# Blocks 1 to 3 of a convolution and feed-forward kernel: turning tiles by transposing transfers instead of on TensorE

## The chip, the cores and the metric

The kernel runs on one core of a Trainium2 chip. The metric is the device time of one execution in microseconds, lower is better; the tables of the profile give times from the start of the span of one profiled execution.

## The reference

One sequence of S = 2048 rows with D = 640 channels (F = 1728 in the feed-forward part). All tensors are bfloat16.

```python
x = A_q
# A: layernorm, short causal filter on k, long causal convolution, gate
q = layernorm(x)
k_shift = sum over t < 4 of k shifted by t rows * shift_k[:, t]
kv = k_shift * A_v
y = causal_convolution(kv, A_ssm_k)          # written with FFTs of length 2*S
y = y + kv * A_ssm_D                         # the skip term
h = x + q * y
# B: layernorm and a gated feed-forward
g = silu(layernorm(h) @ w_gate)
u = layernorm(h) @ w_up
out = h + (g * u) @ w_down
```

## The kernel before, in words

The sequence is cut into four blocks of 512 rows (`j` = 0 to 3); a partition holds four neighbouring rows, so a tile has 128 partitions times four rows (`b`). The channels are cut into two halves of 320 (`c`). For each block and half `conv_c` does the long convolution of the block as a product of spectra:

- `kv_block` (DVE, `tt`, L463): the four-tap filter on k and the product with v, eight products and sums of 128x1280. The rows of k come with three halo rows ahead of them: block 0 loads all channels at once (`load_kv_all`), later blocks by `load_kv`.
- `load_kraw` and `k_natural`: the long filter of the block lies in DRAM with channels as rows. It is loaded so, turned by 12 TensorE transposes of 128x128 (L557), and copied from PSUM to `kt` by ACT (L438) or DVE (L439). For block 0 POOL then adds the skip coefficients to the filter's first row (`dadd`, L564): tap zero of the convolution carries the skip term.
- `fwd`: stage one of the transform on TensorE (L454) and a copy out of PSUM for each `b`, then four shuffles within SBUF (`sh...`, L446, on SP) that bring groups of partitions together. `spec`: stage two. `swapped`: two transfers that exchange the halves of a spectrum. `prods`: products and sums of spectra of this and earlier blocks on DVE. `inv2`, four transfers `rs...`, and `conv_bp` for the way back; `conv_bp` also multiplies by the normed row and adds it to x, and takes the statistics of the second layernorm.
- `ln_bp`: the normed rows `hn` (ACT at L686 or DVE), two row blocks at a time, are turned by 10 TensorE transposes (L848) and copied into `HNT`, which holds channels as partitions.
- `ffn_pair` (seven for a block, L454 with 512 columns): two gate and two up groups of five matmuls into the PSUM tiles `g` and `u`, Silu on ACT (L892), and the product with `u` straight out of PSUM on DVE (`gm`, L463, 128x1024). `ffn_b`: the matmuls of the down projection, the sum with h, and the store.

Every operation goes through `P.op`, which records what it reads and writes. The order on each engine is not found at run time: a packed table `_ORDER` holds, for each operation, its engine and its place, and `replay` and `emit` turn that into five programs, one for each engine, with waits on semaphores. Work of one block's feed-forward and of the next blocks' convolution is interleaved in that order. An engine works strictly in its order: a wait at the head holds everything behind it. That holds for the queues as well: nearly all transfers are issued by SP (L446), a few by POOL and ACT. Buffers come from named pools (`P.pool`), and an operation that reuses a buffer waits for the readers of the earlier tile. The PSUM banks are in two pools of two tiles, `pF` (feed-forward, and part of block 0) and `pC`. Small operations of the layernorm, a power on POOL (L676) among them, stand between the statistics and `hn`.

Of the kernel before, what the change touches and what calls it, by code (L numbers as in the profile page):

```python
# [309 lines left out]
def bass_sequential_preLN__ssm_conv_h3__swiglu_ffn__prompt_kernel(  # L310
# [13 lines left out]
    RESPE = [False, False, False, False]  # L324
    FM = 1664
# [9 lines left out]
    with ExitStack() as es:  # L335
# [14 lines left out]
        def slots(n, size):  # L350
            return [alloc(size) for _ in range(n)]
# [42 lines left out]
        KR01 = P.tile("kraw01", None, WD.base)  # L394
# [7 lines left out]
        P.pool("KRAW", slots(1, 3 * B), True)  # L402
# [9 lines left out]
        P.pool("E", slots(6, HW), True)  # L412
        P.pool("PP", slots(3, HW), True)
        P.pool("EP", slots(3, 2 * CW), True)
# [30 lines left out]
        def dma(subs, kb, reads, writes, prio, eng="sp", after=(), name="", desc=1280, kids=True):  # L445
            fns = [(lambda g, d=d, s=s: g.dma_start(d(), s())) for d, s in subs]  # L446
            engs = {e: {"pool": 0.8, "act": 0.56, "sp": 0.56}[e] * len(subs) for e in ((eng,) if isinstance(eng, str) else eng)}
            return P.op(engs, fns, reads, writes, prio, after=after, dma=(kb, desc), name=name)
# [61 lines left out]
        def load_kv_all(prio):  # L510
            kt, vt = P.tile("kin0", None, GUT.base), P.tile("vin0", None, HNT.base)

            def rows(p0, p1):
                return (lambda: V(kt, 0, 7 * D, p0, p1), lambda: dram(K2, (R * p0 - 3) * D, [[R * D, p1 - p0], [1, 7 * D]]))

            P.op({"pool": 0.3}, lambda g: g.memset(V(kt, 0, 3 * D, 0, 1), 0.0), [], [(kt, "z")], prio, name="kz")
            dma([rows(16, 128), rows(1, 16), (lambda: V(kt, 3 * D, 4 * D, 0, 1), lambda: dram(K2, 0, [[R * D, 1], [1, 4 * D]]))],
                1147, [], [(kt, 0), (kt, 1)], prio, name="kin0", desc=4480)
            dma([(lambda: V(vt, 0, 4 * D), lambda: dram(V2d, 0, [[R * D, 128], [1, R * D]]))], 655, [], [(vt, 0), (vt, 1)], prio + 2, name="vin0", eng=("sp", "act", "pool"), desc=2560)
            for c in range(2):  # L520
                kins[0, c], vins[0, c] = Slab(kt, D, c * CW, c), Slab(vt, D, c * CW, c)

        def load_kv(j, c, prio):
# [3 lines left out]
                750, [], [(kt, 0)], prio, name=f"kin{j}{c}", eng=("sp", "pool"), desc=640)  # L527
            dma([(lambda: V2(vt, 0, CW, 4, CW), lambda: dram(V2d, B * j * D + c * CW, [[R * D, 128], [D, 4], [1, CW]]))],
                426, [], [(vt, 0)], prio + 1, name=f"vin{j}{c}", eng=("sp", "pool"), desc=640)

        def load_kraw(j, c, prio):
            t = kraws[j, c] = KR01 if (j, c) == (0, 1) else P.tile(f"kraw{j}{c}", "KRAW")
            base = c * CW * S + B * j
            dma([(lambda: V2(t, 0, B, 2, B), lambda: dram(A_ssm_k, base, [[S, 128], [128 * S, 2], [1, B]])),
                 (lambda: V(t, 2 * B, B), lambda: dram(A_ssm_k, base + 192 * S, [[S, 128], [1, B]]))],
                393, [], [(t, 0)], prio, name=f"kraw{j}{c}", eng=("sp", "pool") if j else ("act", "sp", "pool"), desc=1024)

        def load_x(j, prio):
            t = xts[j] = P.tile(f"x{j}", "XH")
            dma([(lambda: V(t, 0, 4 * D), lambda: dram(X2, B * j * D, [[R * D, 128], [1, R * D]]))], 655, [],  # L540
                [(t, (b, c)) for b in range(4) for c in range(2)], prio, name=f"x{j}", eng=("sp", "pool"), desc=2560)

        kts = {}
        ktrs, dadds = {}, []

        def k_natural(j, c, prio):
            kr = kraws[j, c]
            kt = P.tile(f"kt{j}{c}", "KT")
            kts[j, c] = Slab(kt, CW, 0, 0)
            pt = P.tile("pKT", cpool(j))  # L550
# [12 lines left out]
            if j == 0:  # L563
                dadds.append(P.op({"pool": 1.0}, lambda g: g.tensor_tensor(out=V(kt, 0, CW, 0, 1), in0=V(kt, 0, CW, 0, 1),  # L564
                                                                           in1=V(DROW, c * CW, CW, 0, 1), op=ALU.add),
                                  [(DROW, 0), (kt, 0)], [(kt, 0)], prio, name="dadd"))

        def fwd(j, nm, srcs, tbpool, upool, prio):

            tbt = P.tile("TB" + nm, tbpool)  # L570
            for b in range(4):
# [6 lines left out]
                pe(fns, CW, len(fns), [(s.t, s.cell) for s, _ in srcs] + [(TAB, 0)], [(pt, 0)], prio, reserve=[(tbt, b)], name=f"s1{nm}b{b}")  # L578
# [3 lines left out]
            for G in range(R):  # L582
# [3 lines left out]
                def src(G=G):  # L586
# [3 lines left out]
                    name=f"sh{nm}G{G}")  # L590
# [9 lines left out]
        def swapped(nm, src, off, h, prio):  # L600
            t = P.tile("W" + nm, "E")
            dma([(lambda: V(t, 0, HW, 0, 64), lambda: V(src, off, HW, 64, 128)), (lambda: V(t, 0, HW, 64, 128), lambda: V(src, off, HW, 0, 64))],
                328, [(src, 2 * h), (src, 2 * h + 1)], [(t, 2 * h), (t, 2 * h + 1)], prio, name=f"sw{nm}", desc=2560)
# [63 lines left out]
        def ln_rstd(l, j, prio, two_pass, bs):  # L667
            lo, hi = bs[0], bs[-1] + 1
            va, y, nm, ng = (tmv(l, j, i)[:, lo:hi] for i in (0, 2, 3, 5))
            if two_pass:  # L670
                src, k1, rd = va, 1.0 / D, [(ST, ("ss", l, j, b)) for b in bs]
            else:
                src, k1, rd = agv(l, j)[:, lo:hi], 1.0, [(ST, ("a", j, b)) for b in bs]
            c1, c3, c4 = ([(ST, ("t", l, j, i, b)) for b in bs] for i in (0, 2, 3))
            vec(0.16, lambda v: v.tensor_scalar(out=va, in0=src, scalar1=k1, scalar2=LN_EPS, op0=ALU.mult, op1=ALU.add), rd, c1, prio, name=f"va{l}{j}")  # L675
            P.op({"pool": 0.4}, lambda g: g.tensor_tensor(out=y, in0=va, in1=stt[:, 288:288 + hi - lo], op=ALU.pow), c1 + [(ST, "half")], c3, prio,  # L676
# [16 lines left out]
        def ln_dve(l, j, prio, bs):  # L693
# [5 lines left out]
            ln_rstd(l, j, prio, False, bs)  # L699

        def ln_x(j, prio):
            for b in range(4):
                for c in range(2):
                    ln_stats(0, j, b, c, xts[j], prio)
            ln_dve(0, j, prio, range(4))

        def kv_block(j, c, prio):
# [12 lines left out]
            def mul(dst, jj):  # L720
                vec(dve2(HW), tt(lambda: v4(dst), lambda: kt.rows(3 - jj), lambda: tapb(jj), ALU.mult),
                    [(kt.t, kt.cell), (kt.t, "z"), (TAPS, jj)], [(dst, 0)], prio, name=f"kvm{j}{c}")
# [15 lines left out]
        def inv2(j, c, G, p1, p2, HTt, prio):  # L738
# [14 lines left out]
            dma([(dst, lambda: V(ht, 0, 2 * CW))], 164, [(ht, 0)], [(HTt, G)], prio + 1, name=f"rs{j}{c}G{G}")  # L753
# [44 lines left out]
        def conv_bp(j, c, bp, HTt, pr):  # L798
# [9 lines left out]
            for k in range(2):  # L808
# [3 lines left out]
            vec(dve1(2 * CW), tt(lambda: V2(ot, 0, CW, 2, CW), lambda: B32x2(pt, CW), lambda: V2(qt, 0, CW, 2, CW), ALU.mult),  # L812
                [(pt, 0), (qt, 0), (qt, 1)], [(ot, 0)], pr, name=f"o{j}{c}{bp}")
# [6 lines left out]
        def conv_c(j, c):  # L820
# [4 lines left out]
            uk = fwd(j, f"K{j}{c}", srcs, "TBK", "UK", pb + 104)  # L825
# [10 lines left out]
        def ln_bp(j, bp, pr):  # L836
            xt = xts[j]
            pt = P.tile("p5", "pC")
            hn = []
            for k in range(2):  # L840
# [3 lines left out]
                norm(lambda t=t: V(t, 0, D), lambda b=b: V(xt, b * D, D), D, 1, j, b, [(xt, (b, 0)), (xt, (b, 1))], [(t, 0)], pr, f"hn{j}{b}")  # L844
            fns = []
# [3 lines left out]
            cells = [(HNT, (d, bp)) for d in range(5)]  # L849
# [5 lines left out]
        def load_weights():  # L855
# [3 lines left out]
            early = [ktrs[0, 1], dadds[1]] + tapms  # L859
# [12 lines left out]
            for w, (wd, o_) in enumerate(((B_w_up, 0), (B_w_gate, 64))):  # L872
                piece([(lambda o_=o_: V2(GUL, o_, 128, 5, 64), lambda wd=wd: dram(wd, FM, [[F, 128], [128 * F, 5], [1, 64]]))], 150,
# [5 lines left out]
        def ffn_pair(j, i, pf):  # L879
# [3 lines left out]
            hr = [(HNT, (d, bp)) for d in range(5) for bp in range(2)]  # L883

            def group(t, bank, w, st, col, cell, prio, reserve):
                fns = [mm(lambda: B32(t, bank, 512), lambda d=d: V(w, d * st + col, 128), lambda d=d: V(HNT, d * 512, 512), d == 0, d == 4)
                       for d in range(5)]
                wr = [(GUL, 0), (GUL, 1)] if w is GUL else [(w, col // 128)]
                pe(fns, 512, 5, hr + wr, [(t, cell)], prio, reserve=reserve, name=f"gu{j}{i}{bank}")
# [9 lines left out]
            if not last:  # L899
# [4 lines left out]
                mul(lambda: V2(GUT, f0 * 512, 512, 2, 512), lambda: B32x2(u, 512), lambda: V2(GUT, f0 * 512, 512, 2, 512), 1024,  # L904
                    [(u, 0), (u, 1), (GUT, f0), (GUT, f1)], [(GUT, f0), (GUT, f1)])
# [31 lines left out]
        def block_j(j):  # L937
# [12 lines left out]
            ln_x(j, pb + (300 if j else 95))  # L950
# [25 lines left out]
    "c-pN~2~?9;7A6bX_k<*5-#0=?LdXVL2q6hcAYn;>up}TNvZ-K4YaONT9a{yg7I(_At+iTgacSM!V%=!bx||lR(rVpxtk$Zis1xjJXL>wSd+$5<-T(dfegFHu"  # L976
    "cYiPd1O&zaq8^PP5O~A@05BN%gn@p|Vt}B>)lnZQ{h#>=Ao%h4!vY|>J!(Hszd{0@1rqQRBp~Luv;Ok%Qx=5*fk%i%*^Lm4iCXjoPm2HmaAX34{}6t*Kh+2D"
    "R4(9ODxV<q#Oi;udMY;XuVX*f3GiF?%nE@<#<M5{{yk~%<LmzY);}%y3%dR7UwlH%Xs7=TYJ&cbe*3eo_+wuH|8MP{iVu9O*Uu9DUMb+Of9go~j7o)K`eH&c"
    "b+pd`Zvd_XP6FgWJzyrF5ilQI71J2g9<vV61fYT<@G-zp%o%_Y@Eo`w8bo=JrBE=qJ$5m~0(*p-hMI#4VNRo=7&n#y8V%YGl7m-*Z-TR8x5W~G?*c=hFTvc{"
    "RB%~r6SyN54EBM)i={*IApqD$hyywuatPvrEP~)62xuGh0Mr1Jz}ujoK-WVXVS8Y=U^ie&_y;gC;zI-rxd(|uZ9)Q29#jT=EqpPYgNPuGBF-QP$Xdh-<SQsW"  # L980
    "dL{Z(%sey#Q-B%3euuq)b>fcU8u5n-6ha&BM_dcRMii2Ih#-g;vJ*mt&Vt^CdSI`^>SLjhPKX3v55Ea7MMx2^A;R#p@G}S+awcj!Di_s)>Ok&5y@q%RxdV}d"
    "grY6zN$8g`^(YNmiyA`7F_$ovm<^b2bT0NGwjQ?wXTW#i?%*cimtut2Tj)%T2Aht12OEnUhZW+l;j;-HgfoQMgrfu&v7dMeFD5M^N#mBq^~Tkaj*-46`QskO"
    "O(MTVz8rTaZZ&xvc`^A*@*}c?(n*m}50MASCW@9)LRmoRqp+!4sHyRTWFTo6(@yH39c52|&4+Zcn>qXFm!*8pPVxojZpb`ZU%Zh~LEl1$GM6)l7-rTx>`s=P"
    "lfx0PQQSq`LmUzh%h&RngoDCX{#?-|ey@Npeo<r-t`QH5XGs=GQ)FN%H{qrXDeX_Vm#{*5T3VJ^ASWim6lqGAcD+KAgi*FC&#OLCYLj;*Z`R<nPSqExR&{G~"
    "TuL6W1HKj*LcWcc;rt*jb|P{k<{a`8dKmW=YCTRtIgjrnEWvN1PNA=+QyG_G$?$pbLHKwC5Q#=X(1Va+s1LgWyAxA^-HEpowiB?#5V4)uM|_h!4gW6wI4&7)"
    "!#CmmxE9<HUP-7S7)et|fH-g53vohXAX?i-+#9DQpCe~dzM(9kOrY+iisN63KN`O%elY$E+S_q6$T;d4Y8k16)JEP-evitHpA~;ReiiKkO+}wW2Qvy77Ur9b"
# [46 lines left out]
```

## Time and profile before

| | |
|---|---|
| median of 13 runs | 325.06 us (323.07 to 328.06) |
| the profiled execution's own time | 323.07 us |
| its span | 321.3 us |
| mean granted TensorE clock | 0.967 |
| HBM read, written | 20.63 MB, 2.62 MB |
| moved by all queues | 49.78 MB |
| transfers issued by SP, POOL, ACT | 217, 13, 4 |
| L557 transposes of the filter | 96, in 8 batches of 12 |
| L848 transposes of the normed rows | 80, in 8 batches of 10 |
| copies of 128x1280 out of PSUM | 10 on ACT (1232 ns), 6 on DVE (820 ns) |

The busy time of an engine is a union of overlapping instructions. For TensorE a busy stretch need not be one at full pace: matmuls are pipelined, and their modelled ends include the way through the array. The number of matmuls in a stretch times their pace in a stretch where nothing holds them says more. A wait is put down to the last of its releasers.

### The profile page before, as it was taken

The numbers are of one execution on the slowest core, as the hardware profiler recorded it, in microseconds if no ns is written. First come the engines' busy times: TensorE is split into PE (matmuls) and PEld (weight loads), VectorE is DVE, ScalarE is ACT, GpSimd is POOL, SyncE is SP. The second block draws the span as 40 slices with busy tenths as digits, with TensorE's granted clock in tenths as the row PEclk, the third lists the DMA queues.
The fourth block names the chain that finished last, engine by engine and source line by source line (L and its number), as shares of the span: only waits on it lengthen the run. The fifth ranks groups of instructions, "written<-read, shape, count | busy, mean of one in ns | idle before, by whom it ended". The sixth has DMA issues, their size and how long they took to land.

```text
span 321.3 us, 4710 instructions
## 1 busy us (share of the span) xinstructions
PE 277.2 (86%) x1650; PEld 156.7 (49%) x1668; DVE 251.2 (78%) x423; ACT 172.8 (54%) x245; POOL 28.5 (9%) x34
## 2 busy tenths in 40 slices
PE   3368487648999698999999999989999999999992
PEld 1243143324454454677555456754444576444671
DVE  1499889897985998999999989989998885123421
ACT  3168579984989475647577577672545302321100
POOL 2110010230240010020000020030001001000000
PEclk9999859976999999999999999999999999999999
DMA  7957969797979468347633601647441110000001
GB/s 204 382 189 228 303 226 286 243 303 228 286 237 289 127 213 228 108 119 241 199 131 104 196 30 71 185 136 226 121 104 42 42 43 10 33 0 0 2 20 62
DMA packets 39355, 49.78 MB, mean 155 GB/s; under 512 B 4466, under 2 KB 33347, under 8 KB 39205
## 3 DMA queue, kind: packets, MB, share of 16 engines
q1 hardware_dynamic: 37682, 45.17, 46.2%
q0 software_dynamic: 1088, 3.88, 4.0%
q10 hardware_dynamic: 562, 0.43, 0.6%
q8 instruction: 13, 0.21, 0.3%
q14 instruction: 10, 0.08, 0.1%
HBM read 20.63 MB, written 2.62 MB: 72 GB/s over the span
## 4 chain that ended last, share of the span: by engine, by line
PE 54%; DVE 15%; ACT 11%; DMA 10%; issue 5%; POOL 2%; SPq 1%; ACTq 0%; DVEq 0%
PE ps L454 52%; DVE sb L463 12%; ACT sb L438 8%; DMA sb<-sb 8%; DMA sb<-in_A_ssm_k_dram 3%; POOL stt L676 2%; DVE stt L660 2%; SPq L446 1%; PE ps L848 1%; PE ps L557 1%; ACT sb L892 1%; ACT sb L686 1%; ACT sb L441 0%; ACT L892 0%; DVE stt L664 0%
## 5 line engine op out<-in xcount | busy, mean ns | idle before, releaser
L454 PE MATMUL ps<-sb 128*128 128x512 bf16 (+2 forms) x978 | 189.7, 343 | 4.0 <-DMA sb<-in_A_shift_k_dram 2.2
L463 DVE TENSOR_TENSOR sb<-sb 128x1280 bf16<-128x1280 bf16 (+1 forms) x208 | 158.5, 793 | 9.3 <-DMA sb<-sb 4.7
L454 PEld LDWEIGHTS ps<-sb 128*128 128x128 bf16 (+1 forms) x996 | 97.0, 98 | 76.6 <-DMA sb<-in_A_shift_k_dram 2.2
L438 ACT ACTIVATE sb<-ps 128x640 bf16<-128x640 f32 (+1 forms) x140 | 97.7, 745 | 53.3 <-PE ps L454 50.1
L454 PE MATMUL ps<-sb,tab 128*128 128x320 bf16 x496 | 94.7, 325 | 24.3 <-DMA sb<-sb 8.0
L463 DVE TENSOR_TENSOR sb<-ps,sb 128x640 bf16<-128x640 f32 (+3 forms) x64 | 60.6, 950 | 37.0 <-PE ps L454 35.7
L454 PEld LDWEIGHTS ps<-sb,tab 128*128 128x128 f16 x496 | 47.2, 103 | 67.3 <-DVE sb L463 11.6
L892 ACT ACTIVATE sb<-ps 128x1024 bf16<-128x1024 f32 (+2 forms) x32 | 29.3, 917 | 41.8 <-PE ps L454 41.7
L686 ACT ACTIVATE sb<-sb,stt 128x320 bf16<-128x320 bf16 (+1 forms) x40 | 28.3, 734 | 17.1 <-DVE stt L678 15.3
L660 DVE BATCH_NORM_STATS2 stt<-sb 128x6 f32<-128x320 bf16 x64 | 29.7, 481 | 0.1
L441 ACT ACTIVATE sb<-ps 128x640 bf16<-128x640 f32 x31 | 21.2, 702 | 12.6 <-PE ps L454 12.5
L676 POOL TENSOR_TENSOR stt<-stt 128x2 f32<-128x2 f32 (+1 forms) x12 | 14.6, 1224 | 149.9 <-DVE stt L675 107.2
L557 PE MATMUL ps<-sb 128*128 128x128 bf16 x96 | 8.5, 253 | 7.3 <-issue 6.0
L439 DVE COPY sb<-ps 128x1280 bf16<-128x1280 bf16 x6 | 4.9, 820 | 10.5 <-PE ps L557 7.9
L557 PEld LDWEIGHTS ps<-sb 128*128 128x128 bf16 x96 | 7.5, 125 | 9.6 <-issue 9.1
L848 PE MATMUL ps<-sb 128*128 128x128 bf16 x80 | 6.9, 242 | 2.6 <-ACT sb L686 2.0
L848 PEld LDWEIGHTS ps<-sb 128*128 128x128 bf16 x80 | 5.5, 109 | 5.0 <-ACT sb L686 3.2
L446 POOL DMA_DIRECT2D sb<-in_A_ssm_k_dram x6 | 4.1, 680 | 41.8 <-PE ps L557 24.2
L664 DVE BATCH_NORM_AGGREGATE stt<-stt 128x2 f32<-128x12 f32 x32 | 5.5, 191 | 0.0
L678 DVE TENSOR_TENSOR stt<-stt 128x2 f32<-128x2 f32 (+1 forms) x12 | 1.8, 155 | 4.5 <-POOL stt L676 4.3
L439 DVE CAST sb<-ps 128x640 bf16<-128x640 f32 x2 | 1.6, 825 | 3.3 <-PE ps L454 3.3
L564 POOL TENSOR_TENSOR sb<-sb 1x320 bf16<-1x320 bf16 x2 | 2.0, 1014 | 17.1 <-DVE sb L439 10.5
(19 smaller groups left out, 19.0 us busy)
## 6 DMA issues: line engine op xcount, KB each, us to landing
sb<-sb SPq DMA_DIRECT2D x160, 160.0 KB, 2.6
sb<-in_A_k_dram SPq DMA_DIRECT2D x6, 560.0 KB, 5.7
sb<-in_A_q_dram SPq DMA_DIRECT2D x4, 640.0 KB, 4.7
out_dram<-sb SPq DMA_DIRECT2D x16, 160.0 KB, 1.9
sb<-in_A_v_dram SPq DMA_DIRECT2D x5, 320.0 KB, 3.7
sb<-in_B_w_gate_dram SPq DMA_DIRECT2D x3, 480.0 KB, 4.6
sb<-in_A_ssm_k_dram SPq DMA_DIRECT2D x4, 256.0 KB, 5.0
sb<-in_A_k_dram SPq DMA_DIRECT2D x1, 980.0 KB
```

The costliest lines, as they stand in the source:

```text
L438: fns = {"act": lambda a: a.activation(out=dst(), in_=src(), func=ACTF.Copy), "dve": lambda v: v.tensor_copy(out=dst(), in_=src())}
L439: "dve": lambda v: v.tensor_copy(out=dst(), in_=src())}
L441: fns = {"act": lambda a: a.activation(out=dst(), in_=src(), func=ACTF.Copy, scale=scale), "dve": lambda v: v.tensor_scalar(out=dst(), in0 ...
L446: fns = [(lambda g, d=d, s=s: g.dma_start(d(), s())) for d, s in subs]
L454: return lambda t: t.matmul(o(), l(), r(), start=st, stop=sp)
L463: return lambda v: v.tensor_tensor(out=o(), in0=a(), in1=b_(), op=op)
L557: return t.transpose(B16(pt, b // 2, (b % 2) * CW + o_, 128), src, V(IDN, 0, 128))
L660: vec(dve1(CW, False), lambda v: v.bn_stats(st6(l, j, b, c), V(xt, b * D + c * CW, CW)), [(xt, (b, c))], [(ST, ("s", j % 2, b, c))], prio, ...
L676: P.op({"pool": 0.4}, lambda g: g.tensor_tensor(out=y, in0=va, in1=stt[:, 288:288 + hi - lo], op=ALU.pow), c1 + [(ST, "half")], c3, prio, ...
L686: "act": lambda a: a.activation(out=dst(), in_=src(), func=ACTF.Identity, scale=rs(l, j, b), bias=tmv(l, j, 3)[:, b:b + 1])},
L848: fns.append(lambda t, k=k, d=d: t.transpose(B16(pt, k, d * 128, 128), V(hn[k], d * 128, 128), V(IDN, 0, 128)))
L892: P.op({"act": act_c(n)}, lambda a: a.activation(out=dst(), in_=src(), func=ACTF.Silu), rd, wr, -1000, name=f"si{j}{i}")
```

## The change

The filters of blocks 1 to 3 and the normed rows of blocks 1 to 3 are turned by `dma_start_transpose` on SP; block 0 keeps the TensorE transposes. A turned filter lands with row 128a + p in partition p, so four more transfers inside SBUF bring it to four neighbouring rows a partition. The skip term of block 0 enters stage one as a matmul with one row. Block 0's own rows of k come in one transfer and the halo rows in two others after it. In `ffn_pair` of blocks 0 to 2, the `u` tile of the first six pairs is copied to SBUF by ACT, and the product reads SBUF. The first pair of block 0 is done in halves of 256 columns, so that its first half needs only the first two row blocks. Some shuffles of block 0 may be issued by ACT, three are. Pools `E` (five buffers, six before), `PP` and `EP` are no longer handed out in strict order, `UT` is new, `KN` replaces `KRAW`. The packed order is a new one: engines and places of operations change throughout, and so do the queues of some loads (x of blocks 0 and 2 and one piece of the transform's table on POOL, most of the weights on SP, issued later).

```diff
+    HNX = [False, True, True, True]
+    SPLIT = ((0, 0),)
+    UEV = [(0, 1, 2, 3, 4, 5), (0, 1, 2, 3, 4, 5), (0, 1, 2, 3, 4, 5), ()]
+    OEV = [False] * 4
...
-        P.pool("KRAW", slots(1, 3 * B), True)
+        P.pool("KN", slots(1, HW), True)
...
-        P.pool("E", slots(6, HW), True)
-        P.pool("PP", slots(3, HW), True)
-        P.pool("EP", slots(3, 2 * CW), True)
+        P.pool("UT", slots(1, 1024))
+        P.pool("E", slots(5, HW))
+        P.pool("PP", slots(3, HW))
+        P.pool("EP", slots(3, 2 * CW))
...
@@ load_kv_all
-            dma([rows(16, 128), rows(1, 16), (lambda: V(kt, 3 * D, 4 * D, 0, 1), lambda: dram(K2, 0, [[R * D, 1], [1, 4 * D]]))],
-                1147, [], [(kt, 0), (kt, 1)], prio, name="kin0", desc=4480)
+            dma([(lambda: V(kt, 3 * D, 4 * D), lambda: dram(K2, 0, [[R * D, 128], [1, R * D]]))], 655, [], [(kt, 0), (kt, 1)], prio, name="kin0", desc=5120)
+            dma([halo(16, 128), halo(1, 16)], 491, [], [(kt, "h")], prio, name="kinh", desc=3840)
...
@@ load_kraw
+            if j:
+                t = kraws[j, c] = P.tile(f"kn{j}{c}", "KN")
+                P.op({"sp": 0.6}, [lambda g: g.dma_start_transpose(V2(t, 0, CW, 4, CW), dram(A_ssm_k, base, [[S, CW], [1, B]]))],
+                     [], [(t, 0)], prio, dma=(328, 1024), name=f"kx{j}{c}")
+                return
...
@@ k_natural
+            if j:
+                dma([(lambda a=a: V2(kt, 0, CW, 4, CW, 32 * a, 32 * a + 32), lambda a=a: V(kr, a * CW, CW)) for a in range(4)],
+                    328, [(kr, 0)], [(kt, 0)], prio, name=f"shk{j}{c}", desc=640)
+                return
...
-            if j == 0:
-                dadds.append(P.op({"pool": 1.0}, lambda g: g.tensor_tensor(out=V(kt, 0, CW, 0, 1), in0=V(kt, 0, CW, 0, 1),
-                                                                           in1=V(DROW, c * CW, CW, 0, 1), op=ALU.add),
-                                  [(DROW, 0), (kt, 0)], [(kt, 0)], prio, name="dadd"))
...
@@ fwd
+                if skip is not None and b == 0:
+                    fns = [mm(lambda T=T, pt=pt: B32(pt, T, CW), lambda T=T: tb(oS1 + T * 128, 128, 0, 1),
+                              lambda: V(DROW, skip * CW, CW, 0, 1), True, False) for T in range(2)] + [
+                           mm(lambda T=T, pt=pt: B32(pt, T, CW), lambda T=T: tb(oS1 + T * 128, 128), lambda: srcs[0][0].row(0), False, True)
+                           for T in range(2)]
...
@@ kv_block
-                    [(kt.t, kt.cell), (kt.t, "z"), (TAPS, jj)], [(dst, 0)], prio, name=f"kvm{j}{c}")
+                    [(kt.t, kt.cell)] + ([(kt.t, "h"), (kt.t, "z")] if jj else []) + [(TAPS, jj)], [(dst, 0)], prio, name=f"kvm{j}{c}")
...
@@ ln_bp
+            if HNX[j]:
+                for k in range(2):
+                    b = bp * 2 + k
+                    P.op({"sp": 0.6}, [lambda g, b=b, k=k: g.dma_start_transpose(V2(HNT, b * 128, 512, 5, 128), V(hn[k], 0, D))],
+                         [(hn[k], 0)], [(HNT, (d, b)) for d in range(5)], pr, dma=(164, 1280), name=f"hx{j}{b}")
+                return
...
@@ ffn_pair
+                cuts = ((0, 256), (256, 512)) if (j, i) in SPLIT else ((0, 512),)
...
+                if i in UEV[j]:
+                    ut = P.tile("ut", "UT")
+                    P.op({"act": act_c(1024)}, lambda a: a.activation(out=V(ut, 0, 1024), in_=B32x2(u, 512), func=ACTF.Copy),
+                         [(u, 0), (u, 1)], [(ut, 0)], -1000, name=f"ue{j}{i}")
+                    vec(dve2(1024), tt(gv, gv, lambda: V(ut, 0, 1024), ALU.mult), [(ut, 0)] + gc, gc, -1000, name=f"gm{j}{i}")
...
 _ORDER = (
-    "c-pN~2~?9;7A6bX_k<*5-#0=?LdXVL2q6hcAYn;>up}TNvZ-K4YaONT9a{yg7I(_At+iTgacSM!V%=!bx||lR(rVpxtk$Zis1xjJXL>wSd+$5<-T(dfegFHu"
+    "c-p;E2UyeB7AJe}y~rYikOcvfkU@4r0)d1iK!C^wCt3&YQH$+U>p-oF+PbxFY^{Qd1MRR+sjW|6>!_oCKC4f0TdDe@wbuIT_xio|y>sq8_uTV8-|zm<?;J1y"
...
```

## The prediction

> **What bounds the kernel now.** I read the page's busy rows first, then the table of stages, then the chain of waits, then the groups by form.
>
> ```profile
> PE 277.2 (86%) x1650; PEld 156.7 (49%) x1668; DVE 251.2 (78%) x423; ACT 172.8 (54%) x245; POOL 28.5 (9%) x34
> PEclk9999859976999999999999999999999999999999
> ```
> ```profile
> 12.00:41.00 29.00, 18.13 (x85) 8.62 (x84) 27.56 (x44) 17.92 (x27) 2.03 (x2) 0.93 0.84 261
> 41.00:73.00 32.00, 21.40 (x120) 10.49 (x119) 29.12 (x64) 28.51 (x44) 6.10 (x7) 0.82 0.87 266
> 73.00:107.00 34.00, 29.59 (x168) 16.10 (x171) 27.90 (x41) 24.76 (x35) 6.16 (x7) 0.92 0.89 257
> 107.00:144.00 37.00, 35.55 (x235) 21.91 (x239) 35.51 (x58) 22.81 (x33) 3.67 (x4) 1.00 0.51 150
> 144.00:183.00 39.00, 38.79 (x239) 22.03 (x241) 38.56 (x58) 25.73 (x33) 0.83 (x2) 1.00 0.57 178
> 183.00:216.00 33.00, 32.07 (x226) 20.94 (x226) 30.86 (x62) 23.52 (x36) 4.74 (x3) 1.00 0.36 110
> ```
> Columns of the stages: length, then PE, weight load, DVE, ACT and POOL busy, granted clock, DMA share, GB/s. From 107 us PE and DVE are both nearly full; before that DVE is, PE is not.
>
> ```profile
> 1.22 8.21 DMA sb<-in_A_ssm_k_dram
> 9.43 1.25 issue
> 10.67 1.46 PE ps L557 x12
> 12.15 0.06 DVE sb L439
> ...
> 33.72 6.10 DMA sb<-sb
> ...
> 111.43 0.67 PE ps L557 x12
> ...
> 146.50 0.56 PE ps L848 x10
> ...
> 250.76 16.80 PE ps L454 x117
> ...
> 281.97 10.74 PE ps L454 x49
> ```
> Busy PE time overlaps itself, so I take the paces of the chain instead: 49 matmuls of 512 columns in 10.74 us is 0.219 us each, 117 (nearly all of 320 columns) in 16.80 us is 0.144; with bare pitches of 0.216 and 0.136, and 0.056 for a transpose (0.56 us for 10), the matmuls counted in each stage come to 9.5 of 29 us, 14.6 of 32, 26.5 of 34, and then 202.8 of the 209 us from 107 to 316. So the kernel is a front of 107 us in which PE is starved of about 54 us, and a stretch in which PE is the limit with DVE close behind. A change gains if it takes work off PE in the stretch, or lets the front hand over earlier.
>
> ```profile
> L463 DVE TENSOR_TENSOR sb<-sb 128x1280 bf16<-128x1280 bf16 x192 | 151.8, 819 | 9.3 <-DMA sb<-sb 4.7 <-PE ps L454 1.6 <-ACT sb L438 1.3
> L463 DVE TENSOR_TENSOR sb<-ps,sb 128x1024 bf16<-128x1024 f32 x24 | 29.3, 1219 | 19.7 <-PE ps L454 19.6
> L892 ACT ACTIVATE sb<-ps 128x1024 bf16<-128x1024 f32 x24 | 24.6, 1024 | 27.8 <-PE ps L454 27.7
> sb<-sb SPq DMA_DIRECT2D x160, 160.0 KB, 2.6
> sb<-in_A_ssm_k_dram SPq DMA_DIRECT2D x4, 256.0 KB, 5.0
> ```
>
> **The change part by part.** Sums are against the profiled execution, 323.07 us (span 321.3, 1.8 around it); it is the fastest of the 13, 2.0 under their median.
>
> *PE.* Six filter batches of 12 transposes (L557) and six of 10 (L848) go: 132 x 0.056 = 7.4 us. Added: four one-row matmuls for the skip term, 4 x 0.136 = 0.5; the first FFN pair in half-width groups, 20 more matmuls over the same columns, about 20 x 0.003 = 0.1. Net -6.8.
>
> *Copies out of PSUM.* Twelve of 128x1280 go (ACT 1.23 us, DVE 0.82 each). All four left stand on ACT: ACT loses ten and gains four, -7.4 us; DVE loses six, -4.9. In blocks 0 to 2, 18 `u` pairs are copied by ACT first (1.024 us as the silu row, +18.4) and multiplied out of SBUF (between 476 ns at 640 and 819 at 1280: 0.68 instead of 1.219, -9.7 us of DVE). With norms and copies that change engine DVE goes to about 239 us, ACT to 182. Neither is a gain by itself: PE stays the limit. It costs nothing in the stretch because ACT is at 62 to 71% there; without that cover each copy would hold a `u` bank 1 us.
>
> *Start.* Before, DVE's first filter-row product stood behind L439, released at 12.15 by the transposes, though its rows were the first on SP's queue. Now that copy is on ACT; 655 KB of own rows come first, halo rows (492 KB) after, and the first product needs only the former. At 204 to 382 GB/s of the first slices that is about 6.5 us: DVE starts some 5.5 us earlier. ACT gets the first filter at about 12 as before, and the two POOL additions of the skip term (1.22 and 0.81 us, PE waited 2.3 us for one) go; the skip row now waits at the last of the first four groups.
>
> *Hand-over.* By the new order PE has done 28.9 us of work ahead of its first L848 batch (70.3 us before), against 25.3; DVE 57.5 against 53.9 us ahead of that norm; ACT 51.0 against 46.8. DVE's 5.5 us earlier start pays 3.6; ACT's 4.2 more is offset by about 3 of earlier start. I leave the batch at 70.3: then 3.6 us more of PE work is behind it, and 6.8 less in all, 10.4 us off the end if the idle behind it stays.
>
> *SP's queue.* 217 issues become 250 (POOL 13 to 9, ACT 4 to 5): +12 `dma_start_transpose`, one a row block, +6 for filters, +24 that spread a turned filter over partitions, -9 others. Between about 25 and 62 us of the order 43 issues become 55: 12 x 0.59 = 7 us more; SP waited 14 us for data in that window, so I charge 1.5. The spreading copies wait on SP for their transpose, and everything queued behind (shuffles on the chain: the 6.10 us piece) waits too. They stand some 6 us behind it. The first gate weights are now issued late, just ahead of use: landing 4.6 us, I charge 1.
>
> *Normed rows through SP.* Before: 0.56 us of transposes and a copy of 0.8 to 1.2. Now: an issue and a landing. Last inverse (o211 at 208.26) to last normed rows (215.0) took 6.9 us in block 2. PE's new order has 12.0 us of matmuls between these points in block 2, 12.5 in block 3, over 23 in block 1: a landing up to about 4.5 us is hidden. [...]
>
> **Two rules weighed.** The trace shows no transposing transfer. The row nearest is 2.6 us for 160 KB, 5.0 for 256 KB from DRAM. [...]
>
> Sum: -10.4 + 1.5 + 1.0 = -7.9: 323.07 becomes 315.2; at the median, 317.
>
> **Rivals.**
> *Slower: transposes serial, the filters' spreading copies block SP.* [...] For: DMA share 0.84 to 0.89 to 107 us, small pieces. Against: the spreading is planned with a gap, and DMA falls to half afterwards. 0.23.
>
> *Half the gain is lost in the front*, by SP or DMA being full: more small pieces (24 x 128 of 640 bytes, transposes in 256-byte rows) at a share of 0.87. The first batch comes 4 us later: 319 own, 321 median. 0.22.
>
> *Nothing left:* the same 8 us later, 325. 0.08.
>
> *More gain:* the first batch comes 5 us earlier, because DVE's start carries through and the clock, 0.82 in 41 to 73, recovers with fewer gaps: 310, 312 at the median. 0.17.
>
> *The forecast*: 0.30.
>
> **How the numbers follow.** Within 0.5% is 1.6 us, about what a measurement of this kernel can tell from no change: 323.4 to 326.7. Faster: 0.30 + 0.17 + 0.22 = 0.69 less a spill of 0.02; same 0.08; slower 0.23 + 0.02 = 0.25. The likeliest three cases alone reach from 308 to 323. The range reaches on to 331, which takes in half of the slow rival, and down to 307.
>
> **What would show it.** Right: transposing transfers landing in 3 to 5 us; the first `gm` product near 75 us; PE idle under 6 us from there; DVE's 1024-wide products near 0.68 us; DVE's first product near 6.5 us. Wrong: SP waiting several us on a filter's transpose with shuffles behind it; PE waiting at a block's first gate matmul for normed rows; a DVE start that stays near 12 us because halo rows or V come late; ACT full between 41 and 107.

## The result, and the profile after

The changed kernel takes 322.82 us (median of 11 runs, 320.44 to 326.09) against 325.83 us for 48 runs of the kernel before: a ratio of 0.9902, with a 95% interval of 0.9874 to 0.993. That is about 3.2 us faster, where the working of the prediction came to 7.9. A second set of runs of the same kernel, on another chip (`f0_changed_again`), gave 0.9863 [0.9814, 0.9912], about 4.5 us. Below, microseconds gained or lost are differences of such ratios times 325.8; the brackets are 95% intervals. The ratios leave disturbed runs out, the medians do not.

The profiled execution of the changed kernel took 324.55 us (span 322.7), 1.7 above its median, and that of the kernel before 323.07, well below its own. Their totals therefore cannot be subtracted: by the two spans the change would be 1.4 us slower. What can be compared is where TensorE (PE) stood still.

The busy rows and the granted clock of the changed kernel:

```profile
PE 269.7 (84%) x1544; PEld 150.3 (47%) x1560; DVE 239.1 (74%) x422; ACT 180.4 (56%) x252; POOL 21.0 (7%) x28
PEclk9996779989999969999799999999999999999998
```

The 132 transposes have gone from TensorE; DVE (VectorE) stands at the 239 us that the prediction worked out, ACT (ScalarE) 1.6 below its 182. Yet PE's share fell as well (86 to 84%), so the work taken off it has in part become idle time. The table of stages, with the columns of the prediction's table, says where:

```profile
12.00:41.00 29.00, 17.70 (x92) 8.43 (x89) 25.25 (x46) 20.67 (x31) 0.06 (x1) 0.82 0.78 227
41.00:73.00 32.00, 21.25 (x110) 10.43 (x111) 24.04 (x41) 25.49 (x42) 0.98 (x1) 0.89 0.89 235
73.00:107.00 34.00, 28.75 (x189) 16.97 (x189) 30.62 (x59) 28.31 (x39) 3.09 (x3) 1.00 1.01 278
107.00:144.00 37.00, 32.71 (x184) 18.77 (x188) 30.35 (x54) 22.11 (x32) 3.79 (x5) 0.91 0.79 216
144.00:183.00 39.00, 35.06 (x194) 19.14 (x195) 32.81 (x55) 22.58 (x30) 2.61 (x3) 0.96 0.68 172
183.00:216.00 33.00, 32.94 (x214) 20.50 (x214) 32.40 (x64) 24.26 (x36) 4.26 (x4) 1.00 0.45 130
```

Before, PE had 235 and 239 matmuls in the two stages from 107 us; now it has 184 and 194, with 2.8 and 3.7 us less of busy time. I count as in the prediction: the recorded matmuls of each stage at their bare paces (0.216 us for 512 columns, 0.136 for 320, 0.056 for a transpose), and the rest of the stage as idle. The paces come out of the timelines: five matmuls of 512 columns take 1.25 us and ten take 2.33, which is 0.216 for one more; four of 320 columns take 0.71 and ten take 1.52, which is 0.135. About 1% of the matmuls are missing from the records, so the last row counts the weight loads instead.

| idle of TensorE, us | before | changed | `f0_changed_again` | `e1_up_early` | `e2_filter_on_pe` | `g2_up_early_rows_on_pe` |
|---|---|---|---|---|---|---|
| 0 to 107 | 55.3 | 53.3 | 52.9 | 53.3 | 47.9 | 55.1 |
| 107 to 144 | 2.0 | 7.4 | 6.9 | 2.0 | 2.4 | 2.1 |
| 144 to 183 | 0.7 | 5.7 | 4.6 | 5.2 | 4.4 | 1.7 |
| 183 to 250 | 3.5 | 3.5 | 3.9 | 3.1 | 4.1 | 3.7 |
| all matmuls at bare pace | 256.0 | 249.2 | | | | |

PE's own work fell by 6.8 us. At 107 us the changed kernel is 8 to 9 us ahead: 6.8 less to do, and 1.5 to 2 more done (the lower figure by weight loads). The next 76 us give up 10.4 us of idle time that the kernel before did not have, and 8.8 in the second profile of the changed kernel, `f0_changed_again`. The chain of waits of the changed kernel (start, length, what; `SPq` is the queue of SP, SyncE, which issues most transfers) shows what begins it:

```profile
102.97 3.97 PE ps L460 x19
...
108.29 0.63 SPq L451
...
108.97 7.43 DMA sb<-in_B_w_up_dram
...
116.44 7.60 PE ps L460 x26
...
124.10 3.53 PE ps L460 x20
...
148.99 7.44 DVE sb L469 x10
...
156.76 11.75 PE ps L460 x53
```

A piece of the up weights is issued at 108.97, lands 7.43 us later, and PE starts behind it. In the timeline of PE, and then of DVE (in brackets the idle time before the instruction, and who ended it), the same place reads:

```profile
116.44 4.45 PE L460 MATMUL ps<-sb 128*128 128x512 bf16 x10 [4.06 <-DMA sb<-in_B_w_up_dram]
...
156.76 3.38 PE L460 MATMUL ps<-sb 128*128 128x512 bf16 x9 [3.07 <-DVE sb L469]
```
```profile
118.79 0.69 DVE L469 TENSOR_TENSOR sb<-ps,sb 128x512 bf16<-128x512 f32 x1 [3.48 <-PE ps L460]
120.19 1.56 DVE L469 TENSOR_TENSOR sb<-sb 128x1280 bf16<-128x1280 bf16 x2 [0.71 <-DMA sb<-sb]
123.87 0.82 DVE L469 TENSOR_TENSOR sb<-ps,sb 128x640 bf16<-128x640 f32 x1 [2.11 <-PE ps L460]
```

PE waits 4.06 us for weights. Its next 10 matmuls take 4.45 us, nearly twice the 2.33 of ten undisturbed ones, and the granted clock shows 0.6 in the slice from 113 to 121 us: TensorE restarts here at about half pace (0.445 us a matmul against 0.233). DVE meanwhile stands still three times for 6.3 us, mostly for PE; from 127.66 us on the chain runs on DVE, until PE waits for DVE at 156.76 and once more restarts slowly (9 matmuls in 3.38 us). In the kernel before, the last two up pieces were issued at 94.3 us, one by SP and one by POOL. Now both stand on SP, at 106.19 and 108.97, just ahead of their use.

The groups, and the transfers, of the changed kernel (queue, kind, KB, median us from issue to landing):

```profile
L469 DVE TENSOR_TENSOR sb<-sb 128x1024 bf16<-128x1024 bf16 x18 | 12.2, 680 | 0.0
L940 ACT ACTIVATE sb<-ps 128x1024 bf16<-128x1024 f32 x18 | 18.4, 1024 | 7.6 <-PE ps L460 5.7 <-DVE stt L687 0.9 <-DVE sb L469 0.8
```
```profile
sb<-sb SPq DMA_DIRECT2D x157, 160.0 KB, 3.2
...
sb<-sb SPq DMA_TRANSPOSE x12, 2.5
sb<-in_A_ssm_k_dram SPq DMA_TRANSPOSE x6, 4.8
```

The turned rows land in 2.5 us and the filters in 4.8: here a transposing transfer is about as quick as a plain one of its size (2.6 us for 160 KB and 5.0 for 256 KB in the profile before).

### The profile page after: what moved, and what is told of

Its sections match the earlier page's. It is cut to its first block, busy times and chain, and to the rows that moved or that the text cites. A ratio compares the mean times of both kernels' runs of the same rounds, so it can differ in the third digit from the quotient of the medians.

```text
span 322.7 us, 4574 instructions
## 1 busy us (share of the span) xinstructions
PE 269.7 (84%) x1544; PEld 150.3 (47%) x1560; DVE 239.1 (74%) x422; ACT 180.4 (56%) x252; POOL 21.0 (7%) x28
## 2 busy tenths in 40 slices
DMA packets 58136, 53.30 MB, mean 165 GB/s; under 512 B 21249, under 2 KB 52418, under 8 KB 58114
## 4 chain that ended last, share of the span: by engine, by line
PE 57%; DMA 19%; DVE 9%; ACT 7%; SPq 3%; issue 3%; ACTq 0%; DVEq 0%
PE ps L460 56%; DMA sb<-sb 11%; DVE sb L469 8%; ACT sb L443 5%; SPq L451 3%; DMA sb<-in_A_ssm_k_dram 3%; DMA sb<-in_B_w_up_dram 2%; DMA tab<-cst_tab 2%; DMA sb<-in_A_v_dram 2%; ACT sb L446 1%; PE ps L573 1%; ACT sb L706 1%; DVE stt L683 1%; ACT L924 0%; ACT sb L924 0%
## 5 line engine op out<-in xcount | busy, mean ns | idle before, releaser
L460 PE MATMUL ps<-sb 128*128 128x512 bf16 (+3 forms) x1000 | 193.9, 343 | 11.0 <-DMA sb<-in_B_w_up_dram 4.1
L469 DVE TENSOR_TENSOR sb<-sb 128x1280 bf16<-128x1280 bf16 (+2 forms) x226 | 167.2, 780 | 26.5 <-ACT sb L443 9.1
L460 PEld LDWEIGHTS ps<-sb 128*128 128x128 bf16 (+1 forms) x1016 | 99.7, 99 | 85.5 <-issue 9.2
L443 ACT ACTIVATE sb<-ps 128x640 bf16<-128x640 f32 (+1 forms) x133 | 90.2, 720 | 51.4 <-PE ps L460 42.1
L469 DVE TENSOR_TENSOR sb<-ps,sb 128x640 bf16<-128x640 f32 (+3 forms) x46 | 38.9, 847 | 44.9 <-PE ps L460 43.5
L940 ACT ACTIVATE sb<-ps 128x1024 bf16<-128x1024 f32 x18 | 18.4, 1024 | 7.6 <-PE ps L460 5.7
L573 PE MATMUL ps<-sb 128*128 128x128 bf16 x24 | 2.7, 310 | 7.1 <-DMA sb<-in_A_ssm_k_dram 7.1
L451 POOL DMA_DIRECT2D sb<-in_B_w_down_dram x4 | 3.1, 768 | 46.7 <-DVE sb L469 36.5
L573 PEld LDWEIGHTS ps<-sb 128*128 128x128 bf16 x24 | 2.5, 145 | 7.7 <-DMA sb<-in_A_ssm_k_dram 7.7
L705 DVE TENSOR_SCALAR sb<-sb,stt 128x320 bf16<-128x320 bf16 (+1 forms) x11 | 4.0, 378 | 2.6 <-DMA sb<-sb 2.6
```

The costliest lines, as they stand in the source:

```text
L443: fns = {"act": lambda a: a.activation(out=dst(), in_=src(), func=ACTF.Copy), "dve": lambda v: v.tensor_copy(out=dst(), in_=src())}
L460: return lambda t: t.matmul(o(), l(), r(), start=st, stop=sp)
L469: return lambda v: v.tensor_tensor(out=o(), in0=a(), in1=b_(), op=op)
L573: return t.transpose(B16(pt, b // 2, (b % 2) * CW + o_, 128), src, V(IDN, 0, 128))
L940: P.op({"act": act_c(1024)}, lambda a: a.activation(out=V(ut, 0, 1024), in_=B32x2(u, 512), func=ACTF.Copy), [(u, 0), (u, 1)], [(ut, 0)], - ...
```

## The experiments

Each kernel starts from the changed one. Its ratio is to the kernel before, run beside it on the same chip. Where only the packed order differs, the places in it (in us of the planned order) are shown.

**The last up weights earlier** (`e1_up_early`, and again as `f1_up_early_again`). The two pieces, columns 768 to 1152 and 1152 to 1664, are issued by POOL behind block 0's second norms.

```
 wu6   sp 87.24  ->  pool 66.0
 wu9   sp 89.58  ->  pool 67.0
```

> The changed kernel with two of the up weight pieces (columns 768 to 1152 and 1152 to 1664) issued by POOL behind the second row norms of block 0, instead of by SP at 106.2 and 109.0 us behind the shuffles. Theory A, late weights: in the changed kernel TensorE waits 4.1 us for the last of these (landed 116.4 us), VectorE is left without work for some 6 us between 115 and 124 us, and sets the pace afterwards up to 157 us; with the pieces there in time 4 to 6 us of the 13 us of TensorE idle between 107 and 183 us go, and the time falls to about 318 us. Theory B, SP and the DMA engines are full up to 107 us whatever is in them: the wait moves to the next late transfer (rows of v, exchange of halves), and the time stays within 1.5 us of 322.8.

> The up pieces early, as run once (318.2 us, ratio 0.9778). If late weights cost the changed kernel 4 to 5 us, it is 4 to 5 us under the changed kernel here too. If the first figure owed to that chip, it is within 2 us of it; the TensorE waits at 112 to 116 us and after would then be made up by others.

Measured 0.9778 [0.9737, 0.9819], median 318.19, and 0.9783 [0.9731, 0.9835], median 318.78; the changed kernel beside the second, `f0_changed_again`, stands at 0.9863. The intervals of the first pair do not touch; those of the second overlap a little.

> The changed kernel, unaltered, beside three of its variants on one chip, since the variants of the first group (318 to 320 us) and of the second (around 324 us) ran on different chips. Expected as before: 322 to 324 us, ratio near 0.990.

The pieces are issued at 76.49 us, and nothing waits for them any more. The stages of `e1_up_early` from 107 us, and its chain there:

```profile
107.00:144.00 37.00, 35.59 (x223) 21.89 (x226) 34.61 (x63) 24.93 (x37) 5.03 (x6) 1.00 0.89 223
144.00:183.00 39.00, 35.88 (x185) 18.53 (x187) 34.38 (x58) 24.48 (x34) 2.88 (x3) 0.96 0.57 151
```
```profile
108.27 8.38 PE ps L460 x44
116.73 0.92 PE ps L460 x5
117.70 8.98 PE ps L460 x49
```

PE has 223 matmuls in the first of these stages instead of 184, the stretch of idle PE and DVE at 112 to 124 us is gone, and the chain lies on PE. Late weights cost the changed kernel 2.6 us (the pair run on one chip) to 4.0 us (the first pair). The edit also takes 1.2 us of issuing off SP; that this is not what helps is seen below, where `e4_spread_on_pool` takes 24 issues off SP for nothing. It does not win everything back: between 144 and 183 us 5.2 us of idle time stay.

**The last up weights later** (`g3_up_later`): `wu6` to 93.5 and `wu9` to 96.0 on SP.

> The changed kernel with the two up pieces moved back by ten issues of SP's queue. Late weights as the cause: TensorE's wait for them grows from 4.1 to 9 us or more, and the time to 325 to 329 us. If the time is set elsewhere and the wait only stands in its place: 322 to 324 us.

Measured 0.9892 [0.9825, 0.9959]: no slower than the changed kernel, so this expectation missed. The reason is in SP's queue and PE's timeline of `g3_up_later`:

```profile
110.03 0.60 SPq L451 DMA_DIRECT2D sb<-in_B_w_up_dram  x1
```
```profile
115.26 4.30 PE L460 MATMUL ps<-sb 128*128 128x512 bf16 x10 [7.71 <-DMA sb<-in_B_w_up_dram]
```

Moved past other transfers in the order, the piece is still issued at 110.0 instead of 109.0. PE happened to reach it earlier, at 107.55, and waited 7.7 us instead of 4.1, with no change in the time. That fits a time set by when the weights land, 115 to 116 us, and not by how long PE is seen to wait. But as the landing hardly moved, the edit does not test what later weights would cost. The slow restart (4.30 us for 10) is no longer after 7.7 us of waiting than after 4.1 (4.45).

**The first gate weights early too** (`g1_gate_early_too`): as `e1_up_early`, with `wg0` from SP at 61.02 to POOL at 37.0.

> The up pieces early (318.2 and 318.8 us, ratio 0.978) and the first gate piece (columns 0 to 384) issued by POOL as well, behind the first row norms. TensorE still waited 1.4 to 2.5 us for gate weights near 78 us. If that wait is on the path as the up pieces' was: 316 to 317.5 us. If VectorE or the transfers within SBUF end the front anyway: within 1 us of 318.5.

Measured 0.9766 [0.9707, 0.9825], median 318.71: the same as `e1_up_early`. PE still waits 1.3 us for gate weights (2.5 in `e1_up_early`). These two, 1.0 to 1.4% below the changed kernel's medians, are the quickest versions found, ahead of both kernels.

**Filters by TensorE again** (`e2_filter_on_pe`): the six later filters are loaded by rows, turned by 72 transposes and copied by ACT.

```diff
 @@ load_kraw
-            if j:
-                t = kraws[j, c] = P.tile(f"kn{j}{c}", "KN")
-                P.op({"sp": 0.6}, [lambda g: g.dma_start_transpose(
...
-            t = kraws[j, c] = KR0[c]
+            t = kraws[j, c] = P.tile(f"kn{j}{c}", "KN") if j else KR0[c]
```

> The changed kernel with the filters of blocks 1 to 3 loaded by rows and turned by TensorE again (12 transposes and one copy of 128x1280 on ScalarE each), SP issuing 2 transfers for a filter instead of a transposing one and four spreading ones. SP: the transposing issue took 1.37 to 3.83 us, median 1.67, and four spreading ones 2.4, against 1.0 for two plain ones: about 3 us of SP less for each, 9 to 12 us in the front. If SP is what holds the front (theory B), the first batch of normed rows (76.6 us) comes 3 to 6 us earlier and the time falls by 2 to 5 us in spite of 4 us more work on TensorE. If late weights are it (theory A), TensorE's 72 transposes and ScalarE's six copies come back and nothing else: 0 to 4 us slower than 322.8.

Measured 0.9824 [0.9784, 0.9863]: 4.0 us more work for PE, and yet about 2.5 us faster than the changed kernel. With six transposing and 24 spreading transfers gone, the last up piece goes out at 104.08 us. The waits of PE between 60 and 250 us in `e2_filter_on_pe` (total, times, longest) hold

```profile
PE ps L460 <- DMA sb<-in_B_w_up_dram: 1.2, 1, 1.2
```

instead of 4.1, and the idle time of PE between 107 and 183 us falls from 13.1 to 6.8 us: in part it mends the same place as `e1_up_early`, by another way. But ahead of 107 us, too, PE stands still 5.4 us less (47.9 against 53.3), which `e1_up_early` does not bring. So the filters' transfers may cost the front something of their own; with one profile, of the fastest run, that is not shown.

**Both** (`e5_up_early_filter_pe`, `f5_up_early_filter_pe_again`): `e1_up_early` and `e2_filter_on_pe` together. And `e6_all_early_filter_pe`, with `wg0` and `wu0` on POOL early as well.

> Both edits that gained, together: the two up pieces issued early by POOL (alone 318.2 us, ratio 0.9778) and the filters of blocks 1 to 3 turned by TensorE (alone 319.8 us, ratio 0.9824; it left a 1.2 us wait for the up piece, against 4.1). If the filters' transfers cost something of their own, in the front (idle of TensorE up to 107 us 47.8 us there, against 53.2 with the weights alone), the two add up in part: 315 to 317 us. If the filters' edit gained only because less traffic let the weights land in time, nothing is added: 318 to 320 us, perhaps above the weights alone for the 4 us of transposes.

> The up pieces early and the filters on TensorE, 323.7 us in the second group. If the two gains are one and the same (weights in time), no better than the kernel with the up pieces early alone: 0 to 3 us slower than it.

> The kernel before this one, and the first gate and up pieces also issued by POOL, ahead of the row norms of block 0. With the up pieces early TensorE still waited 2.0 us at 78 us for the first gate piece. If a late load costs what it delays, 1 to 2 us less than the kernel before this one; if these loads only take the DMA engines from shuffles before 73 us (share 0.99 from 41 to 73 us), as much is lost in the front: the same or 2 us slower.

Measured 0.9895 [0.9841, 0.9949], 0.9895 [0.986, 0.993] and 0.9961 [0.9927, 0.9996]. Beside `f1_up_early_again` on the same chip the 72 transposes cost 3.6 us, near their 4.0 at bare pace. But beside `e2_filter_on_pe`, on another chip, the early pieces made it 2.3 us slower. In `e5_up_early_filter_pe` PE waits 3.4 us for gate weights instead, in its repeat 1.9 and then 3.5 for DVE; bringing the gate weights forward as well was slower still. The profiles show where the early pieces take time: from 73 to 107 us, while they land, PE stands still for 9.2 and 8.5 us against 4.5 in `e2_filter_on_pe`, and from 107 to 183 us, where they could help, only 6.8 us of idle time were left (4.2 and 7.2 with the early pieces). In the changed kernel the early pieces cost the first stretch 1.0 to 2.1 us and win 4.2 to 5.9 behind it. What they hold up was not isolated. Turning the filters by transfer is thus worth 1.5 us (the best version with them, `e1_up_early`, against the best without, `e2_filter_on_pe`) to 3.6.

**Normed rows by TensorE again** (`e3_rows_on_pe`, and with the early weights `g2_up_early_rows_on_pe`).

```diff
-    HNX = [False, True, True, True]
+    HNX = [False] * 4
```

> The changed kernel with the normed rows of blocks 1 to 3 turned by TensorE again (60 transposes, six copies of 128x1280 on ScalarE or VectorE), no transposing transfer for them. The transfers landed in 2.5 us and each took SP 1.23 us instead of the 0.59 forecast; at the blocks' first gate matmuls TensorE waited 3.1 us for VectorE at 156.8 us and about 2 us at 216 to 230 us. If the rows by transfer are worth what was forecast, this is 3 to 4 us slower than 322.8; if SP's time and the landing take it back, within 1 us of it.

> The up pieces early, and the normed rows of blocks 1 to 3 turned by TensorE again. With the weights late this edit changed nothing (322.3 against 322.8 us). If TensorE is the limit once the weights are there, its 60 transposes back cost their 3.4 us: 321 to 323 us. If the transfers cost as much as they save (SP 1.23 us for each, 12 of them, and waits of VectorE and TensorE near 149 and 157 us): within 1.5 us of 318.5.

Measured 0.9905 [0.9871, 0.9939] and 0.9861 [0.9796, 0.9927]. With the weights late (3.3 us of waiting in `e3_rows_on_pe`), 60 transposes more or fewer make no difference; with the weights in time they cost 2.7 to 3.1 us (against `e1_up_early` and, on the same chip, `g1_gate_early_too`), near their 3.4. This is the plainest evidence for the reading: the same saving is worth nothing behind a late transfer and most of its arithmetic without it. Each of these differences is uncertain by some 1.5 to 2.5 us.

**Spreading copies by POOL** (`e4_spread_on_pool`): the 24 `shk` transfers leave SP.

```diff
-                    328, [(kr, 0)], [(kt, 0)], prio, name=f"shk{j}{c}", desc=640)
+                    328, [(kr, 0)], [(kt, 0)], prio, name=f"shk{j}{c}", desc=640, eng=("pool", "sp"))
```

> The changed kernel with the 24 spreading copies of the turned filters issued by POOL instead of SP. Same bytes and pieces on the DMA engines; SP loses 24 issues of 0.59 us and the waits for the filters' landing. Theory B in the form that SP's queue is the limit of the front: first batch of normed rows 3 us earlier or more, time down 2 to 4 us. Theory A, or B in the form that the DMA engines themselves are full (share 0.89 and 1.01 between 41 and 107 us): within 1.5 us of 322.8.

Measured 0.9912 [0.988, 0.9945], and PE still waits 4.0 us for the up piece. The issuing of these 24 is not what costs.

**No copies of `u`** (`e7_no_copy`): `e1_up_early` with 15 of the 18 copies on ACT left out, the product reading PSUM as before.

```diff
-    UEV = [(0, 1, 2, 3, 4, 5), (0, 1, 2, 3, 4, 5), (0, 1, 2, 3, 4, 5), ()]
+    UEV = [(2,), (3,), (0,), ()]
```

> The up pieces early (318.2 us) with 15 of the 18 copies of the up tile by ScalarE left out: VectorE multiplies straight out of PSUM again, at the place of the copy. Tests the step that neither engine's load counts because TensorE is the limit: then within 1.5 us of 318.2. If VectorE is as near to the limit as its 32.2 of 33 us between 183 and 216 us looks, the 15 x 0.54 = 8 us given back to it show: 3 to 7 us slower.

Measured 0.994 [0.9906, 0.9975], some 5 us slower than `e1_up_early`. PE's waits for DVE, first in `e7_no_copy`, then in `e1_up_early`:

```profile
PE ps L460 <- DVE sb L469: 7.8, 11, 2.6
```
```profile
PE ps L460 <- DVE sb L469: 4.2, 3, 2.8
```

and the stage of `e7_no_copy` from 144 us:

```profile
144.00:183.00 39.00, 34.57 (x188) 18.02 (x189) 36.14 (x56) 19.68 (x28) 2.88 (x3) 1.00 0.58 155
```

The copies are needed: without them PE waits for DVE 3.6 us more. DVE is at 36.1 of 39 us in this stage, but that it bounds the stage is not shown: PE stands still there no longer than in `e1_up_early` (4.8 us against 5.2), and 1.9 us longer from 183 to 250 us. (The product also moved, to the place of the copy in the order, so part of the 5 us may be that.)

**The old start** (`e8_old_start`, `f8_old_start_again`): `e1_up_early` with own and halo rows of k in one transfer, and block 0's first filter copied on DVE ahead of its first product.

```diff
-            dma([(lambda: V(kt, 3 * D, 4 * D), lambda: dram(K2, 0, [[R * D, 128], [1, R * D]]))], 655, [], [(kt, 0), (kt, 1)], prio, name="kin0", desc=5120)
-            dma([halo(16, 128), halo(1, 16)], 491, [], [(kt, "h")], prio, name="kinh", desc=3840)
+            dma([rows(16, 128), rows(1, 16), (lambda: V(kt, 3 * D, 4 * D, 0, 1), lambda: dram(K2, 0, [[R * D, 1], [1, 4 * D]]))],
+                1147, [], [(kt, 0), (kt, 1), (kt, "h")], prio, name="kin0", desc=4480)
```

> The up pieces early (318.2 us) with the start undone: own and halo rows of block 0 in one transfer, and the first filter's copy on VectorE ahead of its first product, so that VectorE starts near 13 us instead of 6.8. If the earlier start carries through to the hand-over as forecast (3.6 us of VectorE work done ahead of it), the time rises by 3 to 5 us; if what follows (shuffles, SP) holds the front anyway, by less than 1.5 us.

> The up pieces early and the start undone. If the start carries through, 3 to 5 us slower than the kernel with the up pieces early on the same chip: its first batch of normed rows stood at 80.0 us against 72.6. If it is made up later, within 1.5 us.

Measured 0.9879 [0.9823, 0.9935] and 0.9801 [0.9743, 0.9859]. DVE's first product came at 14.18 and 14.06 us instead of about 6, but the second run is beside `f1_up_early_again` at 0.9783. What the earlier start is worth stays open, between nothing and 3 us.

## Why the prediction had the direction and missed the size

The direction and the mechanism on TensorE held, the size did not: 3.2 us for 7.9.

- **The step that failed** is a term of the sum, the charge of 1 us in "SP's queue": "The first gate weights are now issued late, just ahead of use: landing 4.6 us, I charge 1." The risk was seen, but for the wrong piece and at too low a price. In both profiles of the changed kernel PE's longest wait for weights is that for the last up piece, 4.06 and 4.70 us. Gate weights cost it no wait in the first profile and 2.9 us in the second, and bringing the first of them forward gained nothing (`g1_gate_early_too`). The up piece, issued at 108.97, lands in 7.43 us, directly behind the stage in which the DMA share is 1.01. In the kernel before, an up piece of the same size took 4.5:

```profile
sb<-in_B_w_up_dram SPq DMA_DIRECT2D x1, 640.0 KB, 4.5
```

  The term measures 2.6 to 4.0 us, what early issue brings back. The 10.4 us of the hand-over carried their condition with them, "if the idle behind it stays": the 2.7 us of idle between 107 and 183 became 13.1.
- **A slow restart that was not weighed.** Ten matmuls of 512 columns take 3.75 to 4.45 us after the waits for the up piece in five profiles (3.3 to 7.7 us long), and 2.33 after waits of 0.47 to 1.45 for gate weights in six. There are slow restarts after shorter waits too: once, in `g1_gate_early_too`, ten matmuls took 4.02 us after 1.29, and between 2.4 and 3.3 us it goes either way, here in `f8_old_start_again` and then in `e2_filter_on_pe`:

```profile
90.87 3.88 PE L460 MATMUL ps<-sb 128*128 128x512 bf16 x10 [2.40 <-DMA sb<-in_B_w_gate_dram]
```
```profile
148.41 2.10 PE L460 MATMUL ps<-sb 128*128 128x512 bf16 x9 [3.28 <-DMA sb<-sb]
```

  In these profiles each late landing that made PE wait 3.29 us or more for weights brought 1.4 to 2.1 us of slow matmuls on top of the wait (3.69 to 4.45 less 2.33); a charge of 1 could not hold that.
- **What was right:** PE's saving. It counts 6.8, as forecast, and with the weights in time the kernel is 7.1 to 7.2 us faster. Without any charge for late weights the sum would be 8.9; the 1.7 that are missing fit the 5.2 us of idle that stand in 144 to 183 even then, where DVE is busy for 34.4 of 39 us, but that was not isolated.
- **Wrong in part: "Neither is a gain by itself: PE stays the limit."** `e7_no_copy` says that the copies are needed: without them the kernel is some 5 us slower and PE waits more for DVE. The size of a product out of SBUF, 0.68 us, was right to the digit.
- **The transfers.** They land like the rows nearest (2.6 us for 160 KB, 5.0 for 256 KB): measured 2.5 us for a row block (at most 4.5) and 4.8 for a filter (3.8 to 5.7). No run shows the slower landings behind the slower rival and the 331 us that end the range; with these measured ones that rival falls.
- **SP's own time** went the other way. For each transposing transfer I took the 0.59 us of a plain one. The source lines of the transposing transfers (shortest, median and longest ns, and when) show

```profile
L541 SPq DMA_TRANSPOSE sb<-in_A_ssm_k_dram x6: 1367/1668/3831, 12.2 to 177.7; - x6
```
```profile
L871 SPq DMA_TRANSPOSE sb<-sb x12: 1206/1230/2004, 143.0 to 270.4; - x12
```

  or 1.67 us for a filter and 1.23 for a row block at the median, two to three times what I took. Over 18 transfers the difference is about 14 us of SP's time by the medians. The longest issue, 3.83 us, stands in the queue 12 us ahead of the last up piece:

```profile
96.49 3.83 SPq L541 DMA_TRANSPOSE sb<-in_A_ssm_k_dram  x1
```

  In `e1_up_early` it takes 3.79 us at the same place; in `e2_filter_on_pe` the two plain loads there take 2.13, and the last up piece goes out 4.9 us earlier. That the transposing issues make the up pieces late is thus likely in part, but was not isolated.
- **Start and hand-over.** DVE's first product ran at 6.83 us (forecast 6.5), and the waits for halo rows and for V were small: the timeline of DVE has

```profile
6.83 0.82 DVE L469 TENSOR_TENSOR sb<-sb 128x1280 bf16<-128x1280 bf16 x1 [1.91 <-DMA sb<-in_A_k_dram]
9.24 5.12 DVE L469 TENSOR_TENSOR sb<-sb 128x1280 bf16<-128x1280 bf16 x6 [1.59 <-DMA sb<-in_A_k_dram]
14.88 0.82 DVE L469 TENSOR_TENSOR sb<-sb 128x1280 bf16<-128x1280 bf16 x1 [0.51 <-DMA sb<-in_A_v_dram]
```

  The first batch of normed rows was left at 70.3 us in the forecast, but came at 76.60 here and at 72.7 in `f0_changed_again`, with much the same idle time of PE ahead of 107 us (53.3 and 52.9): it was a poor marker of the hand-over, since PE does other work meanwhile.
- **The half-gain rival** had about the size (321 us at the median, measured 322.8) but not the main cause. It put the loss ahead of 107 us, where PE in fact did 1.5 to 2 us more than before, and `e4_spread_on_pool` took issues off SP for nothing. That the front lost something as well is not ruled out: `e2_filter_on_pe`, without the filters' transfers, has 5.4 us less idle time there. But a profile with them, `g3_up_later`, has 48.7 us too, so this stays open.

## What to carry to other kernels

When a change takes work off the engine that bounds a stretch, ask for every transfer which that stretch needs whether it lands by the new, earlier time; here a load issued "just ahead of use" was the first to be late (PE waited 4.06 us for it), and a further saving on that engine then read as zero. Before a saving is judged, take the late transfer away (here by issuing two weight pieces some 30 us earlier from another queue), for the same 60 transposes were worth nothing with it and about 3 us without. The wait that the profile shows is not the cost: a longer one with the same landing cost nothing more (7.71 us instead of 4.06), and in these traces each one over 3.3 us ahead of the feed-forward's matmuls brought a slow restart of TensorE on top (0.37 to 0.45 us for a matmul of 512 columns, counted over 9 or 10, instead of 0.23).

## What was not expected of the hardware

- A transposing transfer was about as quick to land as a plain one of its size (2.5 us for 128x640 within SBUF, 4.8 us for 320x512 from DRAM; plain ones took 2.6 us for 160 KB and 5.0 for 256 KB before), but held SP's queue two to three times as long (1.23 and 1.67 us at the median against 0.59; once 3.83).
- TensorE's slow restart after waits of 2.4 us and more (once after 1.29), not every time below 3.3, told above: up to 4.45 us for 10 matmuls that take 2.33 otherwise.
- The change multiplies small packets, from 4,466 under 512 bytes to 21,249:

```profile
DMA packets 58136, 53.30 MB, mean 165 GB/s; under 512 B 21249, under 2 KB 52418, under 8 KB 58114
```

  Meanwhile the median landing of the 160 KB shuffles went from 2.6 to 3.2 us. Of the new packets, 8,064 come with the filters by transfer: `e2_filter_on_pe`, without these, has 13,185, and its shuffles land in 2.9 us. Whether the small packets are the reason was not tested.
